# Linear attention and routed experts on one core: the second batch's q and k cast on load and turned by DMA, attention steps in a new order, constant matmuls at the head

## The chip, the cores and the metric

One core of a Trainium2 chip runs the whole kernel. The metric is device time in microseconds (us); before the change the median of three runs is 1014.48 us (1013.58 to 1015.42). The engines work side by side and meet only at semaphores: TensorE (PE; its weight loads are shown apart as PEld), VectorE (DVE), ScalarE (ACT), GpSimd (POOL) and SyncE (SP). SP and POOL issue nearly all DMAs here: SP those that copy or transpose, POOL those that cast from fp32 to bf16 while they load.

## The reference

Two parts follow each other. Attention with a feature map, on 8 batches of 8 heads, 576 tokens of 64 numbers and 128 features:

```python
def phi(x):
    proj = np.einsum('bhsd,df->bhsf', x, w_phi)
    proj = proj - np.max(np.abs(proj), axis=-1, keepdims=True)
    return np.concatenate([np.exp(proj), np.exp(-proj)], axis=-1)
q_p, k_p = (phi(q), phi(k))
kv = np.einsum('bhsf,bhsd->bhfd', k_p, v)
z = np.sum(k_p, axis=2)
num = np.einsum('bhsf,bhfd->bhsd', q_p, kv)
den = np.einsum('bhsf,bhf->bhs', q_p, z)[..., None] + 1e-06
return num / den
```

Its result, as 4608 rows of 512, is the input of a layer of 8 experts, each 512 to 1024 to 512:

```python
P = np.exp(logits)                # x @ w_gate, minus its maximum
for _ in range(8):
    P /= P.sum(1, keepdims=True) + 1e-09
    P /= P.sum(0, keepdims=True) + 1e-09
    P *= N / E
for e in range(E):
    h = np.maximum(x @ w1[e], 0.0)
    out += P[:, e:e + 1] * (h @ w2[e])
```

## The kernel before

**Who decides the order.** The program first collects operations in a planner (`Plan`). Each operation has an engine, an assumed duration, the tiles that it reads and writes, and the ring buffers that it takes. The planner then simulates the engines and emits the instructions in the order of its simulated time: on each engine the operation that can start first goes first, and among equals the one that was collected first. So a list of steps written by hand sets priorities, and the assumed durations set the order too. The chip keeps the emitted order on each engine and each DMA queue.

**Attention.** A batch has four pairs of heads, in two halves of two pairs, and 512 main tokens plus 64 "rest" tokens per head. For every half the loads of q, k and v are one step (`load_qk`, `load_v`). For the matmuls q and k are needed with their 64 numbers along the partitions, so they are turned: into `qkT` for the main tokens, into `rT` for the rest.

For batches 0 and 1, q and k are loaded in fp32 by SP into the accumulator tiles `acc` (which the experts use only later: a batch has two of them, and the rest of both lies in `acc[0]`). `pair_a` turns them with fp32 transposes on TensorE against the identity `identf` (lines 734 to 737), four for k and four for q per pair. DVE copies the turned k and ACT the turned q from PSUM to `qkT`, as bf16. `rest_a` does the same for the rest (lines 660 to 667) with four transposes and a DVE copy.

For batches 2 to 7, POOL loads q and k with a cast to bf16 into `qk` (two buffers) and `qk_r` (two buffers), and SP turns each half with one DMA transpose (`turn_qk`, line 550; `rest_a`, line 669).

The steps, each a letter in the string `order` (line 1085), are:

- `l`: loads of a half; `e`: loads of a rest; `t`: the DMA transpose of a half; `w`: a quarter of the first expert's weights, by POOL. Loads are gated on the latest maxima of steps that stand ahead of them (`gates`).
- `a`: for one pair the turn, the k features (four matmuls, two maxima on DVE, four exponentials on ACT), and v scaled on POOL (line 793).
- `q`, `p`: the maxima and the features of q for a pair; `r`: the rest of a batch.
- `b`, `n`, `m`: the product of k features and v, and the two heads' results.
- `c`: the result turned into `xT`, the experts' input, by TensorE or, for batches 3 to 6, by DMA (line 911); `g`: the rest part of `xT` and the routing logits of a batch.
- `u`, `d`: parts of the first expert's two products (eight matmuls of 512 columns each). A `u` needs all four `xT` blocks of its batch and the weights.

After the string come the routing (line 1129) with the remaining work of the first expert beside it, and then experts 1 to 7, which use fast products with sums. None of this differs between the two kernels, except for how two of its order lists are written out.

**The head.** The first loads of q and k are issued by SP, w_phi comes in two DMAs from ACT's queue (lines 1018 and 1020), DVE clears `wphi2` and two `vrd` tiles (line 1036) and sets `colw` to ones (line 1038).

Of the kernel before, what the change touches and what calls it, by code (L numbers as in the profile page):

```python
# [13 lines left out]
ACT = mybir.ActivationFunctionType  # L14
# [322 lines left out]
def kernel(  # L337
# [11 lines left out]
    nc = tc.nc  # L349
# [26 lines left out]
    colw = const.tile([128, 128], BF16, name="colw")  # L376
# [11 lines left out]
    wphi_f = a_in.tile([128, DF], FP32, name="wphi_f")  # L388
# [3 lines left out]
    vrd = [a_in.tile([128, 2, NP, 2, D1], BF16, name=f"vrd{i}") for i in range(2)]  # L392
# [7 lines left out]
    def pe(cols, fn, r=(), w=(), takes=()):  # L400
        plan.op("PE", max(cols / 2400.0 + 0.0025, 0.031), 0.22, fn, r, w, takes)
# [4 lines left out]
    def dve(el, fn, r=(), w=(), shared=False):  # L406
        plan.op("DVE", el / 960.0 + 0.07, 0.15, fn, r, w, shared=shared)
# [7 lines left out]
    def dma(queue, nbytes, rate, fn, r=(), w=()):  # L415

        speed, unit = LINK.get(rate, (rate, 40))
        if nbytes == 2 << 20:
            speed, unit = 400, 150
        o = plan.op(queue, 0.8 if queue == "POOL" else 0.6, 0.0, fn, r, w, (), nbytes / speed)  # L420
        o.turn, o.unit = rate == 148, unit
# [67 lines left out]
    def new(tag):  # L489
        return R[tag].new()  # L490
# [28 lines left out]
    def load_qk(b, hh, nh, t, r=()):  # L519

        o = hh % 4
        keys = [o // 2] if nh == 2 else [0, 1]
        if b < 2:
            g = t["f"]
            for x, src in ((1, k), (0, q)):
                i = 2 * x + o // 2
                dma("SP", nh << 17, 320, lambda x=x, src=src, i=i: nc.sync.dma_start(
                    out=acc[g][:, i:i + nh // 2].rearrange("p a (h c) -> p (a h) c", h=2),
                    in_=src[b, hh:hh + nh, 0:SM].rearrange("h (p j) d -> p h (j d)", j=NJ)),
                    r, [("acc", g, 2 * x + n) for n in keys])  # L530
            return
        for x, src in ((1, k), (0, q)):
            dma("POOL", nh << 17, 230, lambda x=x, src=src: nc.gpsimd.dma_start(
                out=t["qk"]()[:, x, o:o + nh],
                in_=src[b, hh:hh + nh, 0:SM].rearrange("h (p j) d -> p h (j d)", j=NJ)),
                r, [(t["qk"], x, i) for i in keys])
# [25 lines left out]
    def new_half(b, i):  # L562

        t = {"T": new("qkT"), "v": new("v_m")}
        if b < 2:
            return {"f": 4 - 2 * b - i, **t}
        return {"qk": new("qk"), **t}

    def load_rests(b0, nb, r=()):
        t = {"v": new("v_r"), "b0": b0}  # L570
        if b0 >= 2:
            t["qk"] = new("qk_r")
        for h in range(2):
            rows = slice(h * 64, h * 64 + 64)

            def part(src, h=h):
                return src.rearrange("b (r h) s d -> h s (b r) d", h=2)[
                    h, SM:S, NP * b0:NP * (b0 + nb)]

            for x, src in ((1, k), (0, q)):  # L580
                if b0 < 2:
                    dma("SP", 1 << 16, 150, lambda rows=rows, x=x, src=src, part=part:
                        nc.sync.dma_start(out=acc[0][rows, b0].rearrange(
                            "p (a x d) -> p a x d", a=NP, x=2)[:, :, x], in_=part(src)),
                        r, [("acc", 0, b0, h, x)])
                    continue
                dma("POOL", nb << 16, 90, lambda rows=rows, x=x, src=src, part=part:
                    nc.gpsimd.dma_start(out=t["qk"]()[rows, 0:NP * nb, x, :], in_=part(src)),
                    r, [(t["qk"], h, x)])
            dma("SP", nb << 16, 150, lambda rows=rows, part=part: nc.sync.dma_start(  # L590
                out=t["v"]()[rows, 0:NP * nb], in_=part(v)), r, [(t["v"], h)])
        for b in range(b0, b0 + nb):
            rests[b] = t
# [10 lines left out]
    def mm(out_, lhsT, rhs, start, stop):  # L604
        nc.tensor.matmul(out_, lhsT=lhsT, rhs=rhs, start=start, stop=stop)  # L605
# [45 lines left out]
    def rest_a(b, t):  # L651
# [1 line left out]
        r = {}  # L653
        bi = NP * (b - t["b0"])
        rT = new("rT")
        if b >= 2:
            rk = [(t["qk"], h, x) for h in range(2) for x in range(2)]
        if b < 2:
            ptr = new("PP")
            for pr in range(NP):  # L660
                pe(128, lambda pr=pr: nc.tensor.transpose(
                    ptr()[:, pr * 128:pr * 128 + 128],
                    acc[0][:, b, pr * 128:pr * 128 + 128], identf),
                    [("acc", 0, b, h, x) for h in range(2) for x in range(2)] + ["identf"],
                    [ptr, ("acc", 0, b)])
            dve(512, lambda: nc.vector.tensor_copy(
                out=rT().rearrange("p a b -> p (a b)"), in_=ptr()), [ptr], [rT])
        else:
            dma("SP", 1 << 17, 148, lambda: nc.sync.dma_start_transpose(
                out=rT(), in_=t["qk"]()[:, bi:bi + NP].rearrange("p a b c -> p (a b c)")),  # L670
                rk, [rT])
# [16 lines left out]
        else:  # L688
            mk = [(m, c) for c in range(2 - RM)]
            for c in range(2 - RM):  # L690
                n = NP // 2 * (1 + RM)
# [21 lines left out]
        for h in range(2):  # L713
            rows = slice(h * 64, h * 64 + 64)
            pool(512, lambda rows=rows, h=h: nc.gpsimd.tensor_tensor(
                out=vd[rows, :, :, h, 0:D],
# [8 lines left out]
    def pair_a(b, pr, t):  # L725

        h0 = (2 * pr) % 4
        s = {}
        if b < 2:
            g = t["f"]  # L730
            for x in (1, 0):
                ptr = new("PP")
                i = 2 * x + h0 // 2
                for c in range(4):
                    pe(128, lambda c=c, i=i, ptr=ptr: nc.tensor.transpose(  # L735
                        ptr()[:, c * 128:(c + 1) * 128], acc[g][:, i, c * 128:c * 128 + 128],
                        identf), [("acc", g, i), "identf"], [ptr])
                if x:
                    dve(512, lambda x=x, ptr=ptr: nc.vector.tensor_copy(
                        out=t["T"]()[:, x, 2 * h0:2 * h0 + 4, :].rearrange("p a b -> p (a b)"),  # L740
                        in_=ptr()), [ptr], [(t["T"], x, h0 // 2)])
                else:
                    act(512, lambda x=x, ptr=ptr: nc.scalar.copy(
                        out=t["T"]()[:, x, 2 * h0:2 * h0 + 4, :].rearrange("p a b -> p (a b)"),
                        in_=ptr()), [ptr], [(t["T"], x, h0 // 2)])
# [265 lines left out]


    halves, rests, W = {}, {}, {}
    for b in range(2):
        for i in range(2):
            halves[b, i] = new_half(b, i)
    load_qk(0, 0, 2, halves[0, 0])
    dma("ACT", 1 << 15, 100, lambda: nc.scalar.dma_start(out=wphi_f[0:64, :], in_=w_phi),
        w=["wphi_f0"])
    dma("ACT", 1 << 15, 100, lambda: nc.scalar.dma_start(out=wphi_f[64:128, :], in_=w_phi),  # L1020
        w=["wphi_f1"])
    load_v(0, 0, 2, halves[0, 0])
    pool(300, lambda: make_identity(nc, identf), w=["identf"])
    act(128, lambda: nc.scalar.copy(out=ident, in_=identf), ["identf"], ["ident"])
# [8 lines left out]
    load_qk(0, 4, 4, halves[0, 1])  # L1033
    load_v(0, 4, 4, halves[0, 1])
    for i in range(2):
        dve(450, lambda i=i: nc.vector.memset(vrd[i], 0.0),
            w=[("vrd", i, h, *y) for h in range(2) for y in ((), (1,))])
    dve(128, lambda: nc.vector.memset(colw, 1.0), w=["colw"])
    dma("SP", 1 << 14, 50, lambda: nc.sync.dma_start(
        out=wgate_f, in_=moe_w_gate.rearrange("(c p) e -> p c e", p=128)), w=["wgate_f"])  # L1040
    act(32, lambda: nc.scalar.copy(out=wgate, in_=wgate_f), ["wgate_f"], ["wgate"])
# [12 lines left out]

    def stage_l(n):
        b, i = 1 + n // 2, n % 2
        if b > 1:
            halves[b, i] = new_half(b, i)
        load_qk(b, 4 * i, 4, halves[b, i], gates())
        load_v(b, 4 * i, 4, halves[b, i], gates())  # L1060
# [12 lines left out]
    def stage_g(b):  # L1073
# [2 lines left out]


    at = [0]
    STEPS = {"l": stage_l, "t": lambda n: turn_qk(halves[2 + n // 2, n % 2]), "e": stage_e,
             "w": lambda n: load_w0(n, gates()), "a": stage_a, "q": lambda i: ms[i](), "p": lambda i: qs[i](),  # L1080
             "r": stage_r, "b": stage_b,
             "n": lambda j: kvs[j](0), "m": lambda j: kvs[j](1),
             "c": lambda j: pair_c(j // 4, j % 4, xbs[j]), "g": stage_g,
             "u": lambda i: up0(i // 4, i % 4), "d": lambda i: down0(i // 4, i % 4)}
    order = (
        "lraeaepqbwlqaqawwabwmqlltnrbppnwqbppmrmanbqaqmwwacmpnpbccpwbtcnmqnaqbclupunm"
        "taumquglcapalbcpnqqdcenmucugbblnapmrcqdutabnqpmunpbambccddnqplanmqmducpblttb"
        "augnaqlnrbdcampcadmqeutunqcppmdcaqtdqabpbbmlrqtdnpmuaqualbnagnacctbmqulupran"
        "tdpmtdqcmdnpdabdancpcabbqmpumqbcdgnappqunburqcbugmmnqdcdanumupqbnucmcpnmbddp"
        "bqmpncncubncmmgccg"  # L1090
    )
    for i, n in enumerate(order):
        at[0] = i
# [626 lines left out]
        return {"out": stores, "X1": X1, "Y1": Y1, "Z1": Z1, "X2": X2, "X3": X3, "Z2": Z2, "X4": X4}  # L1720


    ORDER = "X1 x10 w10 x11 X2 x20 y10 x21 Z1 y11 X3 w11 x30 x31 x40 x41 w20 Y1 w21 X4 Z2".split()
    INNER = ("ib1 ia1 ib2 ib3 X1 ia2 ia3 ia5 ia6 ib5 x20 ib6 ia4 x30 ia7 x40 ib4 x21 X2 y10 "
        "ib7 Z1 x31 X3 w20 Z2 y11 w21 x41 Y1 X4").split()
    EARLY = ("w10 x10 X1 w11 y10 x11 x20 Z1 x30 w20 x21 X2 Y1 x31 w21 X3 Z2 X4 x41 y11 x40").split()
    END = "X1 p2 Y1 X2 Z1 p3 X3 Z2 X4 p0 p1".split()
    slots, wait = list(range(6)), []

    def take():  # L1730
# [91 lines left out]
```

## Time and profile before

| What | Value |
|---|---|
| median of three runs | 1014.48 us |
| the profiled execution, its own time | 1013.5 us |
| its span, first to last instruction | 1011.7 us |
| PE busy in the span | 996.5 us |
| first attention matmul | 3.87 us |
| first matmul of the first expert | 44.67 us |
| last turn of a result into xT | 202.09 us |
| first long unbroken run of expert matmuls | from 203.82 us |

The profile is that of one execution on the chip, and its span is a little shorter than the time measured from outside. Matmuls are pipelined, so one matmul's duration is longer than the distance between two; the tables of groups give durations. A line such as "L735 PE" gives the line of the kernel and the engine; "x64" is a count. In the chain of waits each step is followed back from the last instruction to what released it.

| Stretch (us) | DVE busy | ACT busy | POOL busy | DMA share |
|---|---|---|---|---|
| 40 to 50 | 9.93 | 10.00 | 8.11 | 1.33 |
| 50 to 60 | 9.81 | 10.00 | 9.87 | 1.06 |
| 120 to 130 | 9.81 | 9.91 | 6.94 | 1.99 |
| 180 to 190 | 8.95 | 10.00 | 4.31 | 0.34 |

The DMA share is the mean busy share of the core's 16 DMA engines and can pass 1 where transfers of two queues overlap.

### The profile page before, as it was taken

To read this page: it belongs to the slowest core of one execution; us is meant where nothing else is said; L and a number is where in the kernel's file an instruction comes from. 1 tells how busy PE (TensorE), PEld (TensorE's weight loads), DVE (VectorE), ACT (ScalarE), POOL (GpSimd) and SP (SyncE) were. 2 spreads that over 40 slices of the span, in tenths; PEclk is the share of its full clock that TensorE was granted. 3 is DMA by queue.
4 is the path that set the end of the run, shared out by engine and by line. 5 is a ranking of instruction groups with operands and counts; after the bars stand their busy time and mean duration, and the time that the engine had idled before them with its cause. 6 is when DMAs were issued, how large, how long until landed. Compare 5 with 4: busy or idle time off the path is not lost.

```text
span 1011.7 us, 22473 instructions
## 1 busy us (share of the span) xinstructions
PE 996.5 (99%) x8195; PEld 713.6 (71%) x8232; DVE 851.8 (84%) x1979; ACT 797.0 (79%) x1786; POOL 379.7 (38%) x418
## 2 busy tenths in 40 slices
PE   7899999999999999999999999999999999999998
PEld 5666666644566867787777777787778777787775
DVE  8999989986888988789788988898778978888775
ACT  8999999836888787777777777768776877777774
POOL 5778764400133323342333323332333333433333
PEclk9999999999999999999999999999999999999999
DMA  9999989150114411171116121341126111612443
GB/s 253 198 191 177 166 148 134 38 115 1 48 48 96 114 48 48 48 138 56 48 48 117 48 57 52 73 93 48 48 51 144 48 48 48 110 53 69 154 154 142
DMA packets 115087, 93.94 MB, mean 93 GB/s; under 512 B 54432, under 2 KB 97440, under 8 KB 114976
## 3 DMA queue, kind: packets, MB, share of 16 engines
q1 hardware_dynamic: 83024, 68.46, 26.4%
q0 software_dynamic: 31648, 23.86, 17.0%
q8 instruction: 64, 1.05, 0.5%
q14 instruction: 47, 0.39, 0.1%
q10 hardware_dynamic: 304, 0.20, 0.1%
HBM read 92.62 MB, written 14.55 MB: 106 GB/s over the span
## 4 chain that ended last, share of the span: by engine, by line
PE 93%; ACT 3%; DVE 1%; DMA 1%; issue 1%; DVEq 0%
PE ps L1391 42%; PE ps L1400 25%; PE ps L605 17%; PE ps L1487 7%; PE ps L888 2%; ACT k L601 1%; ACT q L601 1%; DMA xT<-wx 1%; DVE wx L597 0%; PE ps L735 0%; DMA acc<-in_k_dram 0%; ACT wx L601 0%; PE ps L917 0%; ACT kr L601 0%; DVE m L597 0%
## 5 line engine op out<-in xcount | busy, mean ns | idle before, releaser
L1671 POOL TENSOR_TENSOR acc<-acc,hx 128x512 f32<-128x512 f32 x186 | 236.0, 1269 | 555.0 <-ACT hx L1668 287.5
L1391 PEld LDWEIGHTS <-hs 128*128 128x128 bf16 x1984 | 194.1, 98 | 56.2 <-issue 0.4
L1462 DVE CUSTOM_DVE_ANT_0 hs<-ps,U 128x512 bf16<-128x512 f32 x252 | 167.0, 685 | 46.6 <-PE ps L1400 29.0
L1668 ACT ACTIVATE hx<-ps,P 128x256 f32<-128x256 f32 x372 | 161.2, 482 | 45.2 <-PE ps L1391 42.3
L1467 ACT ACTIVATE hs<-ps 128x512 bf16<-128x512 f32 x252 | 151.1, 609 | 52.6 <-PE ps L1400 45.8
L1656 DVE SCALAR_TENSOR_TENSOR acc<-ps,P,acc 128x256 f32<-128x256 f32 x372 | 163.2, 476 | 31.8 <-PE ps L1391 30.7
L1391 PEld LDWEIGHTS <-hx 128*128 128x128 bf16 x1488 | 145.5, 98 | 27.1 <-issue 0.6
L1459 ACT COPY ps<-ps 128x512 f32<-128x512 f32 x252 | 146.4, 597 | 12.5 <-PE ps L1487 6.0
L1391 PE MATMUL ps<-hx,hs 128*128 128x256 bf16 x992 | 142.4, 273 | 0.1
L1400 PE MATMUL ps<-X,T 128*128 128x512 bf16 x448 | 131.5, 379 | 0.1
L1499 DVE TENSOR_TENSOR ps<-ps,U 128x256 f32<-128x256 f32 x192 | 75.5, 426 | 36.1 <-PE ps L1487 27.0
L1400 PEld LDWEIGHTS <-T 128*128 128x128 bf16 x672 | 65.7, 98 | 47.1 <-issue 0.6
L1455 ACT COPY U<-ps 128x512 f32<-128x512 f32 x126 | 74.7, 593 | 14.2 <-PE ps L1487 12.8
L1391 PE MATMUL ps<-wx,hs 128*128 128x256 bf16 x560 | 81.5, 273 | 0.0
L1391 PE MATMUL ps<-wx,hx 128*128 128x256 bf16 x496 | 75.9, 273 | 0.0
L1391 PE MATMUL ps<-hx 128*128 128x256 bf16 x496 | 75.9, 273 | 0.0
L1400 PE MATMUL ps<-xT,T 128*128 128x512 bf16 x224 | 72.5, 379 | 0.0
L605 PE MATMUL ps<-xT,w 128*128 128x512 bf16 x271 | 70.1, 379 | 0.6
L605 PE MATMUL ps<-w,hx 128*128 128x512 bf16 x274 | 69.7, 379 | 0.5
L1391 PE MATMUL ps<-w,hx 128*128 128x256 bf16 x432 | 69.8, 273 | 0.0
L1391 PE MATMUL ps<-w,hs 128*128 128x256 bf16 x432 | 64.7, 273 | 0.0
L597 DVE TENSOR_REDUCE m<-ps 128x4 f32<-128x512 f32 x88 | 58.7, 679 | 3.2 <-ACT k L601 1.5
(168 smaller groups left out, 1934.4 us busy)
## 6 DMA issues: line engine op xcount, KB each, us to landing
X<-xd SPq DMA_DIRECT2D x72, 256.0 KB, 2.7
wx<-in_moe_w_dram POOLq DMA_DIRECT2D x8, 1024.0 KB, 12.4
v_m<-in_v_dram SPq DMA_DIRECT2D x15, 512.0 KB, 5.7
out_dram<-acc SPq DMA_DIRECT2D x14, 512.0 KB, 3.2
w<-in_moe_w_dram POOLq DMA_DIRECT2D x6, 1024.0 KB, 10.8
XI<-xd SPq DMA_DIRECT2D x24, 192.0 KB, 2.5
qk<-in_k_dram POOLq DMA_DIRECT2D x12, 256.0 KB, 5.7
qk<-in_q_dram POOLq DMA_DIRECT2D x12, 256.0 KB, 6.9
```

Of the source, the lines that this page charges most:

```text
L605: nc.tensor.matmul(out_, lhsT=lhsT, rhs=rhs, start=start, stop=stop)
L1391: pe(256, lambda i=i, k=k, z=z: nc.tensor.matmul(bank()[:, 256 * i:256 * i + 256], lhsT=lhs(k, i), rhs=rhs(k), start=first and z, stop=k = ...
L1400: pe(512, lambda k=k: nc.tensor.matmul(bank().rearrange("p (a b) -> p a b", a=2), lhsT=lhs(k), rhs=rhs(k), start=first and k == 0, stop=k ...
L1455: act(512, lambda: nc.scalar.copy(out=u[q]().rearrange("p a b -> p (a b)"), in_=w[q]()), bk(w[q]), [u[q]])
L1459: act(512, lambda: nc.scalar.copy(out=to[q](), in_=x[q]()), bk(x[q]), [to[q]])
L1462: dve(515, lambda: nc.vector._custom_dve(ADD_SAT, out=out_(q, i, j), in0=bank[q]().rearrange("p (a b) -> p a b", a=2), in1=u[q](), s0=3.0e ...
L1467: act(512, lambda: nc.scalar.activation(out=out_(q, i, j), in_=bank[q]().rearrange("p (a b) -> p a b", a=2), func=ACT.Relu, bias=0.0, scal ...
L1487: pe(256, lambda: nc.tensor.matmul(at(i, h)(), lhsT=blocks[lhs]()[:, fp], rhs=rhs(), start=start, stop=True, skip_group_check=True), [*xal ...
L1499: dve(256, lambda: nc.vector.tensor_tensor(out=at(i, h)(), in0=at(1, 0)(), in1=s(), op=ALU.add), [k[1, 0], (p5, n)], [k[i, h]])
L1656: dve(320, lambda n=n, ts=ts: nc.vector.scalar_tensor_tensor(out=acc[g][:, ts, 256 * j:256 * j + 256], in0=bank()[:, 256 * n:256 * n + 256 ...
L1668: act(370, lambda n=n: nc.scalar.activation(out=u()[:, n, :], in_=bank()[:, 256 * n:256 * n + 256], func=ACT.Copy, bias=0.0, scale=P[:, 4 ...
L1671: pool(695, lambda: nc.gpsimd.tensor_tensor(out=acc[g][:, 2 * i:2 * i + 2, 256 * j:256 * j + 256], in0=acc[g][:, 2 * i:2 * i + 2, 256 * j: ...
```

## The change

Batch 1 takes the path that batches 2 to 7 take: its q and k are loaded by POOL with a cast into `qk` and `qk_r`, and SP turns them by DMA. Only batch 0 is still turned by TensorE. The steps `t` count from batch 1, so there are 14 instead of 12, and the string of steps is a new one. The assumed duration of an fp32 transpose and of the clearing of `vrd` are raised. At the head `colw` is set first, 26 matmuls of 128 columns on it are put ahead of everything else on TensorE, and w_phi is loaded by one DMA that reads it twice.

```diff
 def load_qk(b, hh, nh, t, r=()):
-        if b < 2:
+        if b < 1:
...
 def new_half(b, i):
-        if b < 2:
+        if b < 1:
             return {"f": 4 - 2 * b - i, **t}
...
 def load_rests(b0, nb, r=()):
-        if b0 >= 2:
+        if b0 >= 1:
             t["qk"] = new("qk_r")
...
-                if b0 < 2:
+                if b0 < 1:
...
 def rest_a(b, t):
-        if b >= 2:
+        if b >= 1:
...
-        if b < 2:
+        if b < 1:
...
-                pe(128, lambda pr=pr: nc.tensor.transpose(
+                pe(256, lambda pr=pr: nc.tensor.transpose(
...
 def pair_a(b, pr, t):
-        if b < 2:
+        if b < 1:
...
-                    pe(128, lambda c=c, i=i, ptr=ptr: nc.tensor.transpose(
+                    pe(256, lambda c=c, i=i, ptr=ptr: nc.tensor.transpose(
...
-    for b in range(2):
-        for i in range(2):
-            halves[b, i] = new_half(b, i)
+    for i in range(2):
+        halves[0, i] = new_half(0, i)
     load_qk(0, 0, 2, halves[0, 0])
-    dma("ACT", 1 << 15, 100, lambda: nc.scalar.dma_start(out=wphi_f[0:64, :], in_=w_phi),
-        w=["wphi_f0"])
-    dma("ACT", 1 << 15, 100, lambda: nc.scalar.dma_start(out=wphi_f[64:128, :], in_=w_phi),
-        w=["wphi_f1"])
+    dve(128, lambda: nc.vector.memset(colw, 1.0), w=["colw"])
+    warm = new("P1")
+    for i in range(26):
+        pe(128, lambda: mm(warm()[:, 0:128], colw, colw, True, True), ["colw"], [warm])
+    dma("ACT", 1 << 16, 100, lambda: nc.scalar.dma_start(
+        out=wphi_f, in_=bass.AP(w_phi.tensor, w_phi.offset, [[0, 2], *w_phi.ap])),
+        w=["wphi_f0", "wphi_f1"])
...
-        dve(450, lambda i=i: nc.vector.memset(vrd[i], 0.0),
+        dve(990, lambda i=i: nc.vector.memset(vrd[i], 0.0),
...
-    dve(128, lambda: nc.vector.memset(colw, 1.0), w=["colw"])
...
 def stage_l(n):
         b, i = 1 + n // 2, n % 2
-        if b > 1:
+        if b > 0:
             halves[b, i] = new_half(b, i)
...
-    STEPS = {"l": stage_l, "t": lambda n: turn_qk(halves[2 + n // 2, n % 2]), "e": stage_e,
+    STEPS = {"l": stage_l, "t": lambda n: turn_qk(halves[1 + n // 2, n % 2]), "e": stage_e,
...
-        "lraeaepqbwlqaqawwabwmqlltnrbppnwqbppmrmanbqaqmwwacmpnpbccpwbtcnmqnaqbclupunm"
-        "taumquglcapalbcpnqqdcenmucugbblnapmrcqdutabnqpmunpbambccddnqplanmqmducpblttb"
-        "augnaqlnrbdcampcadmqeutunqcppmdcaqtdqabpbbmlrqtdnpmuaqualbnagnacctbmqulupran"
-        "tdpmtdqcmdnpdabdancpcabbqmpumqbcdgnappqunburqcbugmmnqdcdanumupqbnucmcpnmbddp"
-        "bqmpncncubncmmgccg"
+        "areqwlpbltalqbamnaaqwpmncwbpwmqbqppnrnbtenatawqqbccbrpmpancllqaqmcpbatpwwbqn"
+        "wlaaebtmunacuumngqmtpncucuuqpultrmbgnqamaulecpcbdmadpqcadlnqpmcbntgdublbmqpu"
+        "qatamnaulnbpnqadrlcpqqudambnmtbmpadadlcqpdbnpcmtaqcmucdnatapubrnuqdcqbnpmcbg"
+        "ptbdpmmulcubunqgcdcmqpuqnnrdurcaqbamqbpcnbddatnqbmpucmunadppgbbacummcnpcmmdd"
+        "ncqupqdbnnpbmccmgncg"
```

Both strings hold the same number of every letter except `t`. `ORDER` and `END`, two lists of the later experts, get a pair of brackets around the same text.

## The prediction

> **What bounds the kernel now.** I read the page's busy times and chain first, then the windows of the first 210 us, the chain of the first 60 us, the engines' timelines there, the answers for the tiles that the change touches, and the DMA issues and waits.
>
> ```profile
> PE 996.5 (99%) x8195; PEld 713.6 (71%) x8232; DVE 851.8 (84%) x1979; ACT 797.0 (79%) x1786; POOL 379.7 (38%) x418
> PE 93%; ACT 3%; DVE 1%; DMA 1%; issue 1%; DVEq 0%
> ```
>
> TensorE ends the kernel. It does nearly the same matmuls whatever the attention order, so only two things move the end: matmul time taken out, and time in which TensorE has nothing to do. Both lie early. The windows (us, busy PE, PEld, DVE, ACT, POOL, each with its count, then clock, DMA share and GB/s):
>
> ```profile
> 0.00:5.00 5.00, 1.13 (x5) 0.88 (x6) 2.38 (x6) 1.58 (x2) 0.69 (x6) 1.00 0.63 173
> 10.00:15.00 5.00, 3.87 (x26) 2.40 (x25) 5.00 (x10) 5.00 (x14) 4.20 (x5) 1.00 1.03 326
> 15.00:20.00 5.00, 4.03 (x41) 2.60 (x40) 4.91 (x8) 5.00 (x16) 4.90 (x10) 1.00 1.36 278
> 30.00:40.00 10.00, 8.52 (x91) 5.90 (x90) 9.63 (x22) 9.93 (x25) 7.28 (x13) 1.00 1.33 176
> 60.00:70.00 10.00, 9.89 (x126) 6.82 (x126) 9.76 (x24) 9.20 (x24) 5.04 (x9) 1.00 1.13 152
> 200.00:210.00 10.00, 9.93 (x85) 5.30 (x85) 8.77 (x23) 3.98 (x8) 1.74 (x2) 1.00 0.54 94
> ```
>
> From 10 to about 45 us ACT and DVE are full and PE is not. Busy PE overstates it, so I counted matmuls by the pitch that unbroken runs show: 1.73/8 = 0.216 us for 512 columns, (0.60 - 0.27)/3 = 0.109 for 256, (0.68 - 0.19)/15 = 0.033 for 65, (0.38 - 0.22)/3 = 0.054 for a bf16 transpose, (0.63 - 0.27)/3 = 0.118 for an fp32 one. That gives 28.7 us of work in the first 45, so 16 us lost; from 45 to 200 only some 4 more are lost. The border is the first expert matmul, at 44.67 us: it needs batch 0's four xT blocks, and from there PE always finds one to fill in. So I ask by how much that border moves. The chain at the head (start, us, what) and the instructions that go:
>
> ```profile
> 0.72 3.01 DMA acc<-in_k_dram
> 3.87 1.10 PE ps L735 x4
> 4.99 0.69 DVE qkT L739
> 5.72 0.23 DVE wphi L1027
> 6.00 1.02 PE ps L605 x4
> 7.04 1.57 ACT k L601 x3
> ```
> ```profile
> L735 PE MATMUL ps<-identf,acc x64: 272/273/472, 3.9 to 34.4; 128*128 128x128 f32 x64
> L739 DVE CAST qkT<-ps x8: 677/680/693, 5.0 to 35.7; 128x512 bf16<-128x512 f32 x8
> L743 ACT CAST qkT<-ps x8: 565/604/726, 6.0 to 37.4; 128x512 bf16<-128x512 f32 x8
> L550 SPq DMA_TRANSPOSE qkT<-qk x12: 1324/2460/5028, 41.7 to 169.8; - x12
> ```
>
> **Taken out.** Of the 64 + 8 fp32 transposes (L735, L661) batch 1 has half: 36 x 0.118 = 4.2 us of PE. They lie before 45 us, where PE has slack, so they are not saved as such. With them go 4 ACT casts at 0.49 in the chain = 2.0 us, and 4 + 1 DVE casts at 0.60 pitch (30.67 to 31.27) = 3.0 us. ACT and DVE take turns in the chain of 7 to 45 us, so the border moves by 2.0 to 3.0; I take 2.5. Nine turns through a PSUM bank go too, at no price I can read. SP issues 8 loads less (0.4 to 1.7 us each); no load is in the chain between 4 and 60 us.
>
> **Head.** The 26 constant matmuls use the idle stretch from 1.0 (after their memset, 0.17 us on DVE) to 3.87. Early PE is slow: tokens x4 take 1.02 us at 6.00, and 0.60 at 10.72; transposes x4 take 1.10, later 0.47 in the chain. If the warm-up reaches both, 0.42 + 0.6 us go; if only the tokens, 0.42; if nothing, none. Constant matmuls at twice the 0.054 pitch last 26 x 0.108 = 2.8 us, to about 3.9, so at worst the first transpose waits 0.1. The page's clock row shows 9 throughout and cannot settle it; the matmul rows do. I take 0.7, with the second w_phi cast leaving the chain (0.23 at 5.72) as part of it. The single w_phi load is covered: the two landed in 3.4 us each, and until 5.7 DVE is on the first cast; beyond that it delays the tokens one for one. The vrd memsets keep their 0.93 us, done before 4; their new cost, like the 256 for transposes, only steers the planner.
>
> The Trainium skill (TensorE: Matmul & The Clock Gate, Part 1) says that the clock is throttled by default and released only after about 3.4 us of sustained activity in a free-running window. The halved early pitch agrees. By it 2.8 us of warm-up would leave the first transposes slow and give about 0.5 instead of 0.7.
>
> **Added.** POOL gets 4 qk issues at 0.8 and 4 qk_r at 0.73 = 6.1 us. From 10 to 45 us it is busy about 28 of 35 us. Counting letters up to the fourth c, the new order has 5 w there instead of 8 (0.6 each), and 14 issues for q and k (three halves, two rests) instead of 8 (two halves, one rest): 6 x 0.77 - 3 x 0.6 = +2.8 us, 31 of 35. It fits; beyond 35 the scaled v (L793, 1.91) would come late, and pair_b's matmuls with it. SP gets two turns of 0.5 MB and one rT turn, each waiting for its POOL load, and v loads queue behind:
>
> ```profile
> qkT<-qk SPq DMA_TRANSPOSE x12, 5.8
> qk<-in_q_dram POOLq DMA_DIRECT2D x12, 256.0 KB, 6.9
> SPq L550 <- DMA qk<-in_q_dram: 31.2, 7, 9.8
> ```
>
> No row shows this so early, hence bounds. The first l is gated on the maxima of pair 0, which ended at 11.4 (reduce x3 at 9.48); two issues to 13; landing 6.9, at 20; turn 5.8, at 26, or 10.1 (the longest), at 30. Batch 0 alone gives ACT 4 x (1.96 + 1.96 + 0.49 + 0.4) + 2.3 = 21.5 us from 6.3, so to 27.8. Bounds: nothing, to 3 us of ACT gap; I take nothing, since the median lands before 27.8. That cover gone, it costs one for one.
>
> The Trainium skill (SBUF — State Buffer, the "DVE blocks DMA" trap) says a load issued by POOL stalls while DVE holds the port that they share. In the trace POOL's issues keep 0.75 to 0.83 us beside DVE work that reads PSUM; by the rule the loads would be later still.
>
> **Order.** Up to the fourth c old and new hold nearly the same: a 8 and 8, b 7 and 7, q 7 and 7, p 8 and 7, n+m 9 and 10, r 3 and 3. A p less is 2.0 us of ACT; an n more is 0.4 + 0.1 + 0.4 = 0.9 us of DVE. Bounds: 0.9 later to 2.0 earlier; I take 0, as the two limits take turns. Steps after that (24 u, 20 d in both) cannot win more than the 4 us lost there.
>
> **Sum.** 2.5 + 0.7 = 3.2 us earlier. Span 1011.7 - 3.2 = 1008.5; the profiled execution took 1013.5, 1.8 more than its span, so 1010.3; the median 1014.48 is 1.0 above the profiled one, so 1011.3. A difference under 0.2% (2 us) is no change here.
>
> **Rivals.**
> 1. More: batch 1 comes later by itself, so batch 0 has ACT and DVE alone. Its DVE work is 24 us (16 + 2 maxima and 5 casts x 0.6, 4 pairs x 2.5 in b, n, m, c), from 5 to 29, and a pair took 6 us more from its first kv matmul to its xT transpose (30.92 to 37.07), so xT could stand at 35 us; PE loses 30% between 25 and 45 (6 of 20), so 9.5 us earlier wins 2.9 more: 1008.4. For it: fewer early loads of w. Against: the new prefix still holds 8 a.
> 2. Nothing: the first u stands at place 84, not 71, with 6.4 us more ACT work ahead. If experts start by the list instead of when xT is there, 6.4 x 0.3 = 1.9 us are given back: 1013.2. Against: in the old trace the first u started 0.5 us after the last xT transpose, not by its place.
> 3. Slower: batch 1's turns come late. Both halves at the longest landing, 4.3 above the median, less 1.8 of cover, lose 6.8 us, against 3.2 won: 1018.1. It decides the sign once the first turn lands after 31 us (27.8 + 3.2). For it: DMA is the busiest of anything from 10 to 60 us (shares over 1), and SP waited 31 us for q. Against: the longest landing twice in a row.
> 4. The turn is not by DMA after all: excluded, batch 1 takes the branch that batches 2 to 7 take.
>
> **Chances.** Forecast 0.42 (own range 1009.5 to 1012.5), rival 1 0.24, rival 2 with other small outcomes 0.14, rival 3 0.20. So faster 0.66, same 0.14, slower 0.20. The range reaches from rival 1, with 2.4 us more of early idle, 1006, to the lower half of rival 3, 1017.
>
> **What would show it.** Right: 32 L735 and 4 L661 records, tokens x4 near 6 us at 0.60, first ACT exponential at 6.3, first expert matmul at 40 to 42 us, the stretch of unbroken expert matmuls from 200.6 (203.8 before). Wrong: ACT idle before 30 us on qkT, SP waiting for qk past 26 us, or more than 4 us of PE loss between 45 and 200.

## The result, and the profile after

The changed kernel takes 1024.35 us (median of 6 runs, 1020.97 to 1025.48) against 1014.66 us for the kernel before in the same session (1013.58 to 1015.42): 1.0091 times as long [1.0075, 1.0106], 9.7 us slower. The forecast was 1011.3. The profiled execution of the changed kernel took 1025.48, its span 1023.7; against the profiled one of before that is 12.0 us more.

The page of the changed kernel, busy times and chain:

```profile
PE 998.6 (98%) x8180; PEld 714.5 (70%) x8222; DVE 850.1 (83%) x1974; ACT 794.5 (78%) x1782; POOL 385.4 (38%) x426
PE 89%; DMA 4%; DVE 2%; ACT 2%; POOL 1%; issue 1%; POOLq 0%; DVEq 0%; SPq 0%; ACTq 0%
```

TensorE still ends the kernel, but DMA, 1% of the chain before, is now 4%. The windows of the changed kernel (us, busy PE, PEld, DVE, ACT, POOL, each with its count, then clock, DMA share and GB/s):

```profile
0.00:5.00 5.00, 3.36 (x30) 3.12 (x30) 2.16 (x4) 1.58 (x2) 0.69 (x6) 1.00 0.55 160
25.00:30.00 5.00, 4.47 (x37) 2.95 (x37) 3.60 (x7) 3.30 (x8) 3.06 (x7) 0.50 1.35 168
24.30:34.50 10.20, 8.96 (x90) 6.46 (x91) 6.93 (x17) 6.96 (x19) 7.40 (x11) 0.50 1.18 200
110.00:120.00 10.00, 6.04 (x29) 2.87 (x29) 5.19 (x10) 5.00 (x13) 5.43 (x8) 0.83 1.30 189
200.00:210.00 10.00, 9.87 (x144) 7.02 (x143) 9.62 (x25) 9.35 (x24) 6.82 (x10) 1.00 0.20 16
```

Before, ACT and DVE were full from 10 to 45 us and TensorE ran short. Now all of them run short: from 25 to 30 us ACT is busy 3.3 of 5 us and DVE 3.6, and from 110 to 120 us TensorE has 40% of its time free and the other three about half. From 24.3 to 34.5 us TensorE is busy for 8.96 of 10.2 us, but the granted clock is 0.50, and its matmuls there take about twice their time. The row of 200 to 210 tells the same: before, ACT was busy there for 4.0 of 10 us, with attention nearly over; now 9.4. Unbroken expert matmuls begin at 217.06 us, 13.2 later than before.

The instructions that were to go did go. The groups of these lines in the changed kernel (durations in ns, least/median/most, first and last start):

```profile
L735 PE MATMUL ps<-identf,acc x32: 272/273/421, 3.8 to 16.8; 128*128 128x128 f32 x32
L743 ACT CAST qkT<-ps x4: 586/706/787, 6.2 to 17.4; 128x512 bf16<-128x512 f32 x4
L550 SPq DMA_TRANSPOSE qkT<-qk x14: 1762/2780/5441, 26.4 to 185.5; - x14
```

Last, what TensorE waits for in the first 210 us (us in total, times, longest), and the chain's longest pieces there (start, us, what), both of the changed kernel:

```profile
PE ps L605 <- DMA qkT<-qk: 6.1, 3, 3.9
PE ps L605 <- DMA rT<-qk_r: 2.2, 1, 2.2
PE ps L735 <- DMA acc<-in_q_dram: 1.1, 1, 1.1
```
```profile
0.72 5.11 DMA wphi_f<-in_w_phi_dram
18.87 5.96 DMA rT<-qk_r
62.31 14.92 DMA qkT<-qk x2
108.95 6.83 DMA qkT<-qk
```

Before, TensorE waited for no turn at all in these 210 us. This is the first story that the profile offers: the new order asks for turned tokens sooner after their load, and they come late. Two pieces of the chain end with such a turn, and TensorE takes the tokens up at once, at 77.28 and 115.83 us. The experiments test this story against others.

A count that the tables below use: TensorE's **lost time** up to 260 us, from where it is full. It is 260 us less its matmuls, each counted once, at the pitch that unbroken runs show at full clock (0.216 us for 512 columns, and so on as in the prediction; 0.056 for 130 columns, 0.028 for 24 and 0.025 for 8). Traces leave out records: those of before show 8195 of 8232 matmuls, all 37 missing ones having 512 columns (pe_neworder's trace below, with none missing, shows which). Their weight loads are in the trace, and by these 35 of them lie before 260 us. With these added, before lost 18.1 us and the changed kernel 33.0 (39 of its 42 missing records lie there). The difference, 14.9, less the 4.2 us of transposes gone, plus 1.4 for the constant matmuls that the count takes as work, is 12.1, against 12.0 us of span. So the whole loss lies before 260 us; behind it both kernels lose 6.0 us.

Most of it lies behind the border that the prediction looked at: from 45 to 200 us before lost 0.5 us, the changed kernel 11.6. The windows of that stretch, first before, then changed, show the same in busy time, without the missing records:

```profile
45.00:200.00 155.00, 152.99 (x1826) 102.40 (x1853) 143.50 (x338) 148.33 (x362) 103.58 (x166) 1.00 0.97 146
45.00:200.00 155.00, 145.28 (x1651) 95.00 (x1678) 134.16 (x310) 141.58 (x349) 101.42 (x163) 0.99 1.06 153
```

Not all lost time is time without work. In the changed kernel the granted clock is 0.50 from 7.2 to 10.6, from 24.3 to 34.5 and from 116.4 to 119.8 us. The matmuls that start there are worth 8.1 us at the full pitch; at half the clock they take about twice that, so by this estimate up to 8.1 of the 33.0 us are the clock. Before, it is 1.00 in all of the first 260 us. (In neither kernel does this row mark the first 5 us, whose matmuls are slow too.)

### The profile page after: what moved, and what is told of

Read it like the earlier page. It is cut to its first block, busy times and chain, and to the rows that moved or that the text cites. A ratio compares the mean times of both kernels' runs of the same rounds, so it can differ in the third digit from the quotient of the medians.

```text
span 1023.7 us, 22425 instructions
## 1 busy us (share of the span) xinstructions
PE 998.6 (98%) x8180; PEld 714.5 (70%) x8222; DVE 850.1 (83%) x1974; ACT 794.5 (78%) x1782; POOL 385.4 (38%) x426
## 3 DMA queue, kind: packets, MB, share of 16 engines
q0 software_dynamic: 34848, 25.04, 18.2%
## 4 chain that ended last, share of the span: by engine, by line
PE 89%; DMA 4%; DVE 2%; ACT 2%; POOL 1%; issue 1%; POOLq 0%; DVEq 0%; SPq 0%; ACTq 0%
PE ps L1392 41%; PE ps L1401 25%; PE ps L605 14%; PE ps L1488 7%; DMA qkT<-qk 2%; PE ps L888 1%; DMA rT<-qk_r 1%; ACT k L601 1%; POOL v L793 1%; ACT q L601 1%; DMA wphi_f<-in_w_phi_dram 0%; DMA xT<-xb 0%; DMA qk_r<-in_q_dram 0%; POOL wx L793 0%; DVE m L597 0%
## 5 line engine op out<-in xcount | busy, mean ns | idle before, releaser
L1456 ACT COPY U<-ps 128x512 f32<-128x512 f32 x126 | 74.7, 593 | 15.4 <-PE ps L1488 12.8
L605 PE MATMUL ps<-xT,w 128*128 128x512 bf16 x268 | 73.5, 381 | 1.8 <-DMA xT<-xb 0.7
## 6 DMA issues: line engine op xcount, KB each, us to landing
wx<-in_moe_w_dram POOLq DMA_DIRECT2D x8, 1024.0 KB, 12.6
```

Of the source, the lines that this page charges most:

```text
L1456: act(512, lambda: nc.scalar.copy(out=u[q]().rearrange("p a b -> p (a b)"), in_=w[q]()), bk(w[q]), [u[q]])
```

## The experiments

Theories: **O**, the turned tokens come late in the new order; **S**, the planner's whole emitted order matters, the old one was good and almost any other is worse; **H**, the head; **P**, the path of batch 1 by DMA costs by itself. All medians, in us, with the difference to the kernel before in the same session (1014.66 beside the changed kernel, 1013.7 to 1014.0 beside the others); the last two columns are TensorE's lost time in the profiled execution:

| kernel | what | median | to before | ratio, 95% | lost to 260 us | of it 45 to 200 us |
|---|---|---|---|---|---|---|
| kernel before | | 1013.7 to 1014.7 | | | 18.1 | 0.5 |
| changed kernel | | 1024.35 | +9.7 | 1.0075 to 1.0106 | 33.0 | 11.6 |
| h_old | changed, old head | 1026.98 | +13.3 | 1.0109 to 1.0151 | 36.2 | 11.0 |
| pe_neworder | changed, batch 1 by TensorE | 1024.07 | +10.4 | 1.0083 to 1.0120 | 26.1 | 10.3 |
| dma_oldorder | before, batch 1 by DMA | 1032.63 | +18.9 | 1.0161 to 1.0202 | 41.4 | 16.3 |
| b_head | before, new head | 1019.68 | +6.0 | 1.0038 to 1.0086 | 26.5 | 8.7 |
| fixhead | old emitted order held, new head | 1015.81 | +1.8 | 1.0006 to 1.0024 | 19.1 | 2.2 |
| fixwarm | same, two w_phi loads | 1014.45 | +0.5 | 0.9998 to 1.0016 | 17.4 | 0.9 |
| fixdma | old emitted order held, batch 1 by DMA | 1030.49 | +16.5 | 1.0128 to 1.0173 | 34.6 | 5.7 |
| fixdma2 | same, first turn early | 1024.86 | +11.0 | 1.0091 to 1.0126 | 32.4 | 4.2 |
| b_costs | before, two kinds of assumed duration | 1018.25 | +4.2 | 1.0030 to 1.0067 | 23.0 | 5.6 |
| b_null | before, one assumed duration | 1020.35 | +6.4 | 1.0053 to 1.0078 | 24.0 | 5.8 |
| b_null3 | before, another one | 1023.11 | +9.2 | 1.0077 to 1.0104 | 27.1 | 9.8 |
| a_null | changed, b_null's edit | 1026.52 | +12.6 | 1.0103 to 1.0134 | 35.8 | 13.7 |
| a_hoist | changed, loads of batches 2 to 7 earlier | 1025.36 | +11.4 | 1.0102 to 1.0132 | 31.9 | 11.1 |
| a_hoist1 | changed, all these loads earlier | 1029.04 | +15.1 | 1.0132 to 1.0168 | 36.4 | 12.7 |
| a_twow | changed, two w_phi loads | 1025.32 | +11.3 | 1.0106 to 1.0137 | 32.0 | 9.0 |
| late_all | changed, planner takes landings 2 us later | 1119.43 | +105.4 | 1.1018 to 1.1048 | 32.1 | 9.5 |

**One part at a time, the planner free to reorder.** h_old puts the old head into the changed kernel, b_head the new head into the kernel before.

```diff
-    dve(128, lambda: nc.vector.memset(colw, 1.0), w=["colw"])
-    warm = new("P1")
-    for i in range(26):
-        pe(128, lambda: mm(warm()[:, 0:128], colw, colw, True, True), ["colw"], [warm])
-    dma("ACT", 1 << 16, 100, lambda: nc.scalar.dma_start(
-        out=wphi_f, in_=bass.AP(w_phi.tensor, w_phi.offset, [[0, 2], *w_phi.ap])),
-        w=["wphi_f0", "wphi_f1"])
+    dma("ACT", 1 << 15, 100, lambda: nc.scalar.dma_start(out=wphi_f[0:64, :], in_=w_phi),
+        w=["wphi_f0"])
+    dma("ACT", 1 << 15, 100, lambda: nc.scalar.dma_start(out=wphi_f[64:128, :], in_=w_phi),
+        w=["wphi_f1"])
```

> The changed kernel with the head of before: no constant matmuls, two loads of w_phi, colw set late. Theory H (the head is the cause: the first exponential of ACT moved from 7.04 to 8.24 us, and the single w_phi load landed 5.1 us after its issue) expects most of the 9.7 us back, 1015 to 1017. Theory P (batch 1's turn by DMA comes too late, whatever the order) and theory O (the new string of steps gives loads and turns too little lead) expect only the head's own 1 to 1.5 us, 1022 to 1024.

> The kernel of before with the new head alone (26 constant matmuls, one w_phi load, colw set first). H expects 1020 to 1024. P and O expect the head's own cost: the first exponential 1 us later, 1014.5 to 1016.5.

The old head did not help the changed kernel: 13.3 us over before, instead of 9.7. The new head alone cost 6.0. Two edits of one small thing, and neither sum fits: both gave the planner another order for everything behind, so they say nothing of the head alone. For H an order held fixed was needed.

pe_neworder turns batch 1 by TensorE again, in the new string without its first two t; dma_oldorder turns it by DMA in the old string, with a t put in at places 12 and 25.

```diff
-        if b < 1:
+        if b < 2:
             ptr = new("PP")
...
-    STEPS = {"l": stage_l, "t": lambda n: turn_qk(halves[1 + n // 2, n % 2]), "e": stage_e,
+    STEPS = {"l": stage_l, "t": lambda n: turn_qk(halves[2 + n // 2, n % 2]), "e": stage_e,
```

> The changed kernel with batch 1 turned by TensorE again as before (36 fp32 transposes and their 9 casts are back); new head, new string of steps without its first two t. P expects the time of before or near it, 1013 to 1017, as nothing waits for batch 1's DMA transposes. O expects that the waits for qkT near 62 to 77 and 109 to 116 us stay, and 1019 to 1025. H expects 1022 to 1025.

> The kernel of before with batch 1 loaded with a cast and turned by DMA, under the old string of steps with two t put in (at places 12 and 25), old head. P expects a gap of ACT before 35 us of 4 us or more and 1018 to 1024. O expects no wait over 1 us for qkT after 45 us and 1010 to 1016. H expects 1011 to 1014.

pe_neworder is the run that decides most. It has none of batch 1's turns, and it is as slow as the changed kernel (+10.4 and +9.7, intervals overlapping). So batch 1's late turns are not what makes the change slow. Nearly all that pe_neworder loses beyond the kernel before lies between 45 and 200 us (10.3 against 0.5); up to 45 us it loses 16.0, before 17.5. The same pair also shows what the path does: the changed kernel has 4.2 us less matmul work and loses 6.9 us more (33.0 against 26.1), 5.6 of it in the first 45 us. The work saved is real, and the waits for turns and the halved clock around them use it up: pe_neworder's clock is 1.00 in all of the first 260 us (0.998 to 1.000 over its four executions), that of the changed kernel's six executions 0.990 to 0.997. How much of the 6.9 us is wait and how much clock was not separated, and the two profiled executions lie 2.4 us apart where the medians differ by 0.3. The path in the old string, +18.9, was no better.

**The emitted order held.** In these, the planner plans the kernel before as it was, and the edit changes only what an operation emits. fixhead emits the constant matmuls ahead of everything and both halves of w_phi in one load; fixwarm leaves w_phi's two loads.

```diff
         with tc.manual_schedule():
+            self.first()
             for o in done:
...
+    def first():
+        nc.vector.memset(warmw, 1.0)
+        for i in range(26):
+            mm(ps[:, 0:128], warmw, warmw, True, True)
...
-    dma("ACT", 1 << 15, 100, lambda: nc.scalar.dma_start(out=wphi_f[0:64, :], in_=w_phi),
+    dma("ACT", 1 << 15, 100, lambda: nc.scalar.dma_start(
+        out=wphi_f, in_=bass.AP(w_phi.tensor, w_phi.offset, [[0, 2], *w_phi.ap])),
         w=["wphi_f0"])
-    dma("ACT", 1 << 15, 100, lambda: nc.scalar.dma_start(out=wphi_f[64:128, :], in_=w_phi),
-        w=["wphi_f1"])
+    dma("ACT", 1 << 15, 100, lambda: None, w=["wphi_f1"])
```

> The kernel of before with its instructions in exactly the old order, the new head put in ahead by hand: 26 constant matmuls first, one w_phi load in place of the first of two. Theory S (what costs is that any change of the planner's inputs gives another order of instructions, and the old order was fitted to the chip) expects the head's own price and no more, 1013 to 1015.5. Theory H (the head itself costs the 6 us that it cost alone) expects 1018 to 1021.

> The kernel of before with its order held, 26 constant matmuls first, w_phi by two loads as before. If the single w_phi load was the head's whole price (fixhead took 1.8 us more), the warm clock brings 0.3 to 0.8 us: 1013 to 1014. If the constant matmuls cost, 1015 to 1016.

The head by itself costs 1.8 us, and with two loads 0.5, an interval that holds no change. So the single load is what costs. The head of the changed kernel on its engines, in order of time (start, us, what, idle time before and what ended it):

```profile
0.72 1.14 ACTq L1021 DMA_DIRECT2D wphi_f<-in_w_phi_dram  x1
...
3.79 0.61 PE L735 MATMUL ps<-identf,acc 128*128 128x128 f32 x4
...
5.93 0.46 DVE L1029 CAST wphi<-wphi_f 64x128 bf16<-64x128 f32 x2 [2.63 <-DMA wphi_f<-in_w_phi_dram]
...
6.42 0.69 DVE L739 CAST qkT<-ps 128x512 bf16<-128x512 f32 x1
...
7.17 1.04 PE L605 MATMUL ps<-wphi,qkT 128*128 128x256 bf16 x4 [0.98 <-DVE qkT L739]
```

The one load lands 5.1 us after its issue, where each of the two landed in 3.4. DVE takes its work in order and stands at w_phi's cast until 5.93, with the cast of the first turned tokens queued behind, so the tokens start at 7.17 instead of 6.00, and the first exponential at 8.24 instead of 7.04. By then the granted clock has fallen to 0.50 (7.2 to 10.6 us), and the tokens take 1.04 us, as slow as before. In fixwarm's timeline of TensorE the same matmuls come in time:

```profile
1.04 2.96 PE L607 MATMUL ps<-warmw 128*128 128x128 bf16 x26 [1.04 <-DVE warmw L1016]
...
5.88 0.60 PE L607 MATMUL ps<-wphi,qkT 128*128 128x256 bf16 x4 [0.33 <-DVE wphi L1035]
```

They take 0.60 us, as forecast, and the first exponential starts at 6.52. But this half microsecond does not reach the end.

fixdma gives batch 1's loads to POOL, casting into a view of the buffers that the fp32 tokens had, at the places where SP's loads stood; each half is turned by one DMA where its first cast stood, and the 36 transposes and 9 casts go. fixdma2 also moves the first half's loads up behind POOL's first operation, and its turn ahead of the half's v load on SP.

```diff
+                if b == 1:
+                    dma("SP", nh << 17, 320, lambda x=x, src=src: nc.gpsimd.dma_start(
+                        out=cast_view(g)[:, x, o:o + nh],
+                        in_=src[b, hh:hh + nh, 0:SM].rearrange("h (p j) d -> p h (j d)", j=NJ)),
+                        r, [("acc", g, 2 * x + n) for n in keys])
+                    continue
...
-                    pe(128, lambda c=c, i=i, ptr=ptr: nc.tensor.transpose(
+                    pe(128, lambda c=c, i=i, ptr=ptr: None if b == 1 else nc.tensor.transpose(
...
-                    act(512, lambda x=x, ptr=ptr: nc.scalar.copy(
+                    act(512, lambda x=x, ptr=ptr: turn_once(g, t) if b == 1 else nc.scalar.copy(
```

> The kernel of before with everything in the old order, but batch 1's loads are cast by POOL into the same tiles, at the places where SP's loads stood, each half is turned by one DMA transpose at the place of its first cast, and the 36 TensorE transposes with their 9 casts are left out. S expects a gain or no loss, 1009 to 1015. Theory P (the DMA path is what costs, through turns that land too late) expects TensorE waiting for qkT before 45 us for over 4 us and 1018 to 1026.

> As fixdma (old order held, batch 1 turned by DMA), with batch 1's first loads put at POOL's first free place (right after its first small operation, near 8.5 us, not at 11.5) and its first turn put ahead of the v load that SP waited with until 18 us. If the DMA path costs because the first turn lands too late (34.7 us in fixdma), the turn lands near 24 us, TensorE's 7.9 us wait for qkT goes, and the time is 1012 to 1020. If the path costs through its load on POOL and the DMA engines, 1024 to 1031 as before.

The first answer of fixdma is one wait (TensorE's timeline):

```profile
34.68 0.39 PE L632 MATMUL ps<-wphi,qkT 128*128 128x256 bf16 x1 [7.90 <-DMA qkT<-acc]
```

With the first turn as early as the queues allow, that wait shrinks, and others come up (what TensorE waits for in fixdma2, first 210 us):

```profile
PE ps L777 <- DMA acc<-in_k_dram: 5.4, 2, 3.8
PE ps L645 <- DMA qkT<-acc: 4.3, 1, 4.3
PE ps L777 <- DMA acc<-in_q_dram: 2.7, 2, 1.8
```

The turn, issued at 19.67, landed only at about 31.4, and batch 0's own loads now landed late: TensorE waits 1.6 us for k at 15.4 and 1.8 for q at 18.2. From 20 to 30 us the 16 DMA engines' share is 1.68. The granted clock is 0.50 for some 20 of the first 47 us in both. So P holds in the old order as it is: 16.5 or 11.0 us go, for 4.2 us of TensorE's work. That the early traffic has no room for batch 1's loads and turns fits this, but how much is late data and how much the clock was not separated.

**Only the order.** b_costs changes two kinds of assumed duration in the kernel before, b_null and b_null3 one each. The instructions and the data they move are the same; the planner only puts them in another order. The two of b_costs are the ones that the change itself raises.

```diff
-        dve(272, lambda: nc.vector.tensor_copy(
+        dve(290, lambda: nc.vector.tensor_copy(
             out=kv().rearrange("p a b c -> p (a b c)"), in_=pkv()[:, 0:4 * D1]), [pkv], [kv])
```
```diff
-            dve(5 * D1, lambda: nc.vector.tensor_tensor(
+            dve(5 * D1 + 10, lambda: nc.vector.tensor_tensor(
                 out=num(), in0=num(), in1=s["r"]()[:, h, :, None].to_broadcast([128, 5, D1]),
```
```diff
-                pe(128, lambda pr=pr: nc.tensor.transpose(
+                pe(256, lambda pr=pr: nc.tensor.transpose(
...
-                    pe(128, lambda c=c, i=i, ptr=ptr: nc.tensor.transpose(
+                    pe(256, lambda c=c, i=i, ptr=ptr: nc.tensor.transpose(
...
-        dve(450, lambda i=i: nc.vector.memset(vrd[i], 0.0),
+        dve(990, lambda i=i: nc.vector.memset(vrd[i], 0.0),
```

> The kernel of before with nothing changed but two durations that the planner assumes (256 instead of 128 columns for an fp32 transpose, 990 instead of 450 elements for clearing vrd): the same instructions in another order. S expects 1017 to 1023, as for other changes of the order. H and P expect 1013 to 1015.5.

> The kernel of before with one assumed duration changed that no part of the change touches (the copy of kv, 290 instead of 272 elements): the same instructions in another order. S expects 1016 to 1022, like the 1018 of the other change of assumed durations alone. If the old order is nothing special, 1012 to 1016.

> The kernel of before with another assumed duration changed a little (the scaling of the first product, 335 instead of 325 elements). Theory S expects 1016 to 1022 again. If the two other changes of an assumed duration were bad luck, 1012 to 1016.

> The changed kernel with one assumed duration changed that no part of the change touches (the copy of kv, 290 instead of 272 elements). If the new string was fitted to the chip as the old one was, another order loses 4 to 6 us more, 1028 to 1031. If it is one order among many, 1021 to 1028 on either side of 1024.

Three edits that change nothing physical cost 4.2, 6.4 and 9.2 us. The loss lies in the same stretch as pe_neworder's: 5.6, 5.8 and 9.8 us from 45 to 200 us, against 0.5. In b_costs and b_null the first expert matmul comes at 51.07 and 51.68 us instead of 44.67. b_null3 shows where such time goes. One of its windows, in the columns used above, and what its engines wait for in that window:

```profile
80.00:100.00 20.00, 17.33 (x185) 11.15 (x187) 15.03 (x35) 14.99 (x36) 15.55 (x25) 0.91 1.37 187
```
```profile
ACT em L601 <- POOL m L791: 2.9, 1, 2.9
PE ps L605 <- ACT q L601: 2.5, 2, 2.1
DVE rec L901 <- PE ps L888: 2.1, 1, 2.1
```

No transfer is late for TensorE here. ACT stands behind a small POOL operation, TensorE behind ACT, DVE behind TensorE, and all of them are short of work at once, as in the changed kernel from 110 to 120 us. In the kernel before TensorE is busy 19.8 us of the same 20, and no wait there is over 0.9 us. a_null gives the changed kernel the same edit as b_null: +12.6 against +9.7, so its order is not a specially good one either, but one of many.

**Theory O, directly.** a_hoist keeps the changed kernel's emitted order but moves POOL's q and k loads of batches 2 to 7 up by as much as 8 us of planned time (not ahead of the turn that frees their buffer); a_hoist1 moves batch 1's too. late_all tells the planner that data of a DMA can be used 3.0 us after its transfer, not 1.0. a_twow gives the changed kernel's held order the two w_phi loads.

```diff
+        for o in sorted(self.loads, key=done.index)[4:]:
+            p = done.index(o)
...
+            t = self.at[id(o)] - 8.0
...
+            n = next((i for i in range(floor, p) if self.at[id(done[i])] >= t), p)
+            done.insert(n, done.pop(p))
```
```diff
-                o.end = landed[0] + 1.0
+                o.end = landed[0] + 3.0
```
```diff
+    def both():
+        for h in (0, 64):
+            nc.scalar.dma_start(out=wphi_f[h:h + 64, :], in_=w_phi)
```

> The changed kernel with its order held on every engine, except that POOL's loads of q and k from batch 2 on stand earlier in its queue, by up to 8 us of the planner's time (not ahead of the turn that frees their buffer). Theory O (loads with too little lead: TensorE reaches q and k that are not yet turned) expects the waits for qkT at 62 to 77 and 109 to 116 us to fall from 6 to below 2 us, and 4 to 8 us less than the changed kernel, 1016 to 1020. Theory S (any order that was not fitted on the chip loses about as much) expects no gain over 2 us, 1022 to 1026.

> As the last one, with batch 1's loads earlier too (at 10 to 14 us instead of 18.7 to 21.9, ahead of most of the rest's loads). P and O expect the first turn of batch 1 to be issued near 20 instead of 26.4 us, the ACT gap between 20 and 40 us to shrink from 4 us to under 2, and another 1 to 3 us less than the run with the later batches alone. S expects no gain.

> The changed kernel with one constant of the planner changed: it assumes that a DMA's data can be used 3.0 us after its transfer instead of 1.0. Theory O (the order lets TensorE reach turned q and k before they have landed, and all behind it waits) expects the waits for qkT and rT, 10 us in the changed kernel, to fall below 4, and 1014 to 1019. S without O expects just another order, 1019 to 1029, waits as long as before.

> The changed kernel with its order held and w_phi loaded by two DMAs again; the constant matmuls stay. The head's own price was the single load, which landed 5.1 us after its issue (3.4 for each of two): the first exponential at 7.0 to 7.4 instead of 8.2 us, and 1 to 2 us less, 1022 to 1023.5. If the constant matmuls are what costs, no change.

a_hoist did what it was made for: TensorE's wait for qkT fell from 6.1 to 1.7 us. Little came of it. A wait for xT (3.0 us, 0.7 in the changed kernel) took its place, that for rT stayed (1.9 and 2.2), and the lost time stayed too, 31.9 against 33.0. With batch 1's loads hoisted as well it rose to 36.4. late_all is a miss as an experiment: the constant holds for every DMA, so the expert stage was planned anew as well, and 95 of its 105 us were lost behind 260 us. Of its attention one thing can be read: waits for turns are gone from the top of TensorE's list, yet the lost time up to 260 us is 32.1, and unbroken expert matmuls begin at 215.7 us instead of 217.06. a_twow won nothing: its wait for qkT is 7.4 us, so what the head gives, a later wait takes.

So late turns are where much of the changed kernel's lost time shows, but not what makes the kernel slow. Take them away, and time is lost elsewhere.

## Why the prediction was wrong, step by step

**Order: the step that failed.** The prediction compared how many steps of each kind stand ahead of the fourth c, took 0 for the order up to there, and said of everything behind it that it "cannot win more than the 4 us lost there". That bounds the gain and leaves the loss open, and the loss is what came: 11.1 of the 14.9 us more of lost time lie between 45 and 200 us. The 4 us were not there to win either: with every matmul counted once and the missing records put in, before lost 17.5 us up to 45 us and 0.5 from 45 to 200, not 16 and 4. The raised durations, of which the prediction says that their cost "only steers the planner", were put at nothing as well; they alone cost 4.2 us in the old string (b_costs). pe_neworder (+10.4) less the head held alone (+1.8) puts the new order, string and durations together, at about 8.6 us; the path in that order adds 9.7 - 10.4 = -0.7, within the intervals' width. The parts do not quite add (h_old, with the old head, is slower, not faster), because each edit gives a new order of its own. The nulls show that a string with the same letters can cost that much: in the kernel before, the handover between four nearly full engines leaves TensorE hardly a gap behind 45 us, and reorderings that no count of steps can tell from it lose 4 to 9 us. The counts of letters were right and told nothing.

**Head: a wrong sign.** Forecast 0.7 earlier, measured 1.8 later (fixhead). The prediction named the limit, DVE busy until 5.7 us and every delay beyond it one for one, and took 3.4 us for the landing from the two small loads. The one load took 5.1 to 5.5. The gains it counted exist: the first four transposes take 0.61 us instead of 1.10, and with two loads the tokens take 0.60 instead of 1.02. They bring at most half a microsecond at 7 us and nothing that can be measured at the end.

**Taken out: right in number, nothing in time.** 32 records of L735 and 4 of L661 are left, and 4.2 us of work are gone from TensorE. The 2.5 us by which the border was to move did not appear: one expert matmul stands alone at 29.80 us, and the steady sequence starts at 46.46, not at 42.

**Added: the landing was mis-sized.** The first turn was to land at 26 us. POOL could issue batch 1's loads only at 18.65 to 21.87 us, not near 12, since four loads for the rest tokens (10.5 to 15.5 us), a weight load and the scaled values stood ahead of them in its queue. SP issued the turn at 26.43; it landed at 31.5, and its tokens were used from 33.43. So the condition of rival 3, a first turn that lands after 31 us, was just met. ACT idled 2.7 us before 26.70, but behind the turn of batch 1's rest, which landed at 24.8. The rival's price, 1018.1, and its decision of the sign were not borne out: without any of these turns (pe_neworder) the kernel is as slow. What the prediction's sum did not have at all is the clock, which falls to 0.50 around the late turns. Its test "more than 4 us of PE loss between 45 and 200" came true with 11.6 us.

The prediction set the Trainium skill's rule on POOL's loads under DVE work (SBUF — State Buffer, the "DVE blocks DMA" trap) beside its rows. No stall shows: the four issues take 0.74 to 0.83 us each, as before. They were late because of what stood ahead of them in POOL's queue.

**Rivals 1 and 2.** Neither came. The transposes left TensorE and batch 1 came later by itself, but xT did not come earlier.

**Not settled.** Whether some order with batch 1 turned by DMA beats the kernel before: no run of this study had one fitted on the chip, and 4.2 us of matmul time are there to be won. How the order's price divides between the string and the two raised durations: no run changed the string alone. And why a given order loses: in the replanned kernels the loss is spread over many waits. That the old order was fitted to the chip's times is an inference from ten reorderings of either kernel's plan, all 4 us or more slower; it was not shown.

## What to carry to other kernels

Where a planner or a list fixes the order of several nearly full engines, test an edit with the emitted order held, and beside it a null edit that changes an assumed duration alone: here the nulls spread over 4 to 9 us of 1014, more than any part of this change could win. A bound on what a reordering can win is no bound on what it can lose. And before two loads are made one, or a turn is given to a DMA, ask which in-order queue stands behind the landing, with the landing time of that very size in that stretch. Behind a new wait of TensorE look at the granted clock too: here 10 us at half the clock began with a wait of 2.2.

## What the hardware showed that was not expected

- **A load with a repeated source lands later than two.** Both halves of w_phi in one 64 KB load: 5.1 us (changed kernel) and 5.5 (fixhead) from issue to landing; as two loads of 32 KB, 3.4 each. A plain load of 64 KB was not run, so the repeat and the size are not told apart.
- **The clock comes and goes within a few microseconds.** In the changed kernel the granted clock falls to 0.50 at 7.2, 24.3 and 116.4 us; in the 3.4 us before each fall TensorE was busy for 1.28, 1.13 and 0.57 us. In the kernel before it is 1.00 in the first 260 us. The Trainium skill (TensorE: Matmul & The Clock Gate, Part 1) puts a fall to half the clock behind an idle window of about 3.4 us; the longest wait that the trace names around the second fall is 2.2 us, so here less than 3.4 us of unbroken idle time was enough. It also says that the clock rises after some 3.4 us of sustained work; here 2.8 us of constant matmuls made the first transposes fast. The fall is not needed for the loss: pe_neworder and b_null show 1.00 in all windows from 20 to 120 us. But in the changed kernel it takes part of what the path saves.
- **Landing times were longer where the share was high.** In fixdma2, with a share of 1.68 from 20 to 30 us, the two turns of half a batch up to 40 us landed after 7.7 and 11.7 us, against a median of 4.8 over the whole changed kernel.
